# Long convolution with expert selection: eight places for x, a PSUM room, and two half blocks summed on VectorE

## The chip, the cores and the metric

One core of one Trainium2 chip. The metric is device time in microseconds (us) of one execution. The kernel before has a median of 868.43 us over three runs (866.48 to 869.74).

## What is computed

```python
def _attn_ref(x, v, pos_emb, w1, w2):
    h_mlp = np.maximum(pos_emb @ w1, 0.0) @ w2
    h_filt = h_mlp * np.exp(-0.01 * pos)[:, None]
    u = x * v
    Uf = np.fft.rfft(u, n=2 * S, axis=1)
    Hf = np.fft.rfft(h_filt, n=2 * S, axis=0)
    y = np.fft.irfft(Uf * Hf[None], n=2 * S, axis=1)[:, :S, :]
    return x * y                      # (4, 12608, 128), f32

def _moe_ref(x, w_gate, w1, w2, capacity):
    scores = np.einsum('bsd,d->bs', x, w_gate)
    out = x.copy()
    for b in range(B):
        top_idx = np.argpartition(-scores[b], capacity)[:capacity]
        ...
        out[b, top_idx] = x[b, top_idx] + g[:, None] * ye
    return out
```

The long convolution of `x * v` with a generated filter is multiplied by `x`. Every row of that product is given a score (its dot product with `w_gate`), the 128 best rows of each batch go through a small network, and their result is added to them.

## The kernel before

After the filter's transform (to about 106 us) the four batches are worked through in 128 groups of four channels, 32 groups per batch. A group goes through a forward transform (TensorE, lines L436 and L278), a product with the filter's transform (VectorE, L442 to L457, and GpSimd, L463 and L464) and a first backward transform (TensorE, L273), whose result ScalarE copies into the big tile `ay` (L487, L488). The loop over `t` keeps groups at several stages in flight: the backward transform belongs to group `t - 3`. So one turn of the loop issues, on TensorE, L273 of an old group, then L278 of group `t`, then L436 of group `t + 1`; on ScalarE L487 and L488, then L281 (the copy `qs` of one half of L278's result), then two L438.

After the last group of a batch the loop runs `P1.run`, called the run below: it finishes the batch. The batch has 16 blocks of 8 columns, worked in the order `ORD`, each as two half blocks `h` of 4 columns:

```python
HB = 4
LA = range(32 - 12, 32 - 2)
ORD = (0, 9, 1, 10, 2, 3, 11, 4, 12, 5, 6, 13, 7, 14, 8, 15)
NL, NM = 28, 7
DW = (2, 14)
```

For each half block TensorE makes the last backward transform into one of four PSUM tiles (`mm`, L553 and L557). VectorE multiplies it with x, in place of x (`fin`, L568). Then the product is multiplied with the gate's weights into a "room" `wx` (`weigh`, L602: on VectorE, or on GpSimd for the far columns), and ScalarE adds up each of the room's four columns with an activation that has an accumulator, in place (`sums`, L612): its result is the score of 128 rows. The rooms for VectorE's L602 are four, used in turn (`self.wx`): two in the arena's region `wx`, one in `te`, one in `ht`. The sums of the last four half blocks of a batch are kept for later (`late`) and issued in three lots by the next batch's first groups, behind the two L438 of a group; after them `mask` (L616) sets invalid scores aside and the selection of the 128 best begins, in the background of the next batch's groups. Its last step before it uses TensorE is a chain on VectorE (L616, L783, L779), then ScalarE (L780, L781). In the last batch nothing is late, and the last two half blocks (30, 31) are summed on VectorE itself by four `scalar_tensor_tensor` with an accumulator each (L586).

Where x lies: block number `i` of the order lies in place `i % 7`. Five places are a region of their own (`xa`), two (`XE`) lie over the buffers `qs` and `mt` of the groups. The first five blocks are loaded in halves ahead, one half in each of the groups `LA` (20 to 29) of the batch; two more when the run starts; and the load of block `i + 6` (L530) is issued by SyncE behind the store of block `i` (L591), and waits until the store of block `i - 1`, whose place it takes, has landed. SyncE issues all transfers of the kernel in one order, so a load that waits holds the stores behind it. Since `qs` and `mt` share bytes with the two `XE` places, the first L281 after a run waits for the store of the last block that lay in the first `XE` place: block number 12 of the order; VectorE's first L450 waits for the same.

Of the kernel before, what the change touches and what calls it, by code (L numbers as in the profile page):

```python
# [23 lines left out]
NG = 32  # L24
HC = 4 * N1
# [4 lines left out]
HB = 4  # L30
# [13 lines left out]
LA = range(32 - 12, 32 - 2)  # L44
# [8 lines left out]
DW = (2, 14)  # L53
OFF, _o = {}, 0
for _n, _k, _w in (("te", 2, 2 * HC), ("qs", 2, HC), ("mt", 1, 2 * HC), ("ws", 1, 888), ("yz", 2, 2 * HC), ("sd", 2, 2 * HC),
                   ("ht", NH, 2 * HC), ("xa", NX, 8 * D), ("wx", 2, HB * D), ("cm", 2, 2 * NC * D), ("x", NU, XC), ("", 1, 2), ("v", NV, XC)):
    OFF[_n] = (_o, _k, _w)
    _o += _k * _w
ARENA = _o
XE = [OFF["qs"][0] + k * 12 * D for k in range(2)]  # L60
CE = [o + 8 * D for o in XE]
POS0, HID0 = 0, PJ * N1
# [109 lines left out]
def hyena_moe(ctx, tc, xg, x2, pos, bw, ww, wg, mw1, mw2, fo, fc, c1, gx, cf, ci, wm, tk, out):  # L172
# [34 lines left out]
    def gap(k, n):  # L207
        return bank2[k].rearrange("p (c x) -> p c x", c=2)[:, :, HC:HC + n]
# [303 lines left out]
    class P1:  # L512
        def __init__(self, b):
            self.b = b
            self.sc = small([128, NJ], f"sc_{b}", tag="sc")
            self.xa, self.s4, self.cm = {}, {}, {}
            self.mul = None
            self.hbs = hbs
            self.more = iter(CB)
            self.pw = self.nw = 0  # L520
            self.late = []

        def load_a(self, i, a=0, z=8):
            if i < len(ORD):
                k = ORD[i]
                j0, j1 = blocks[k]
                z = min(z, j1 - j0)
                o = i % (NX + len(XE))
                self.xa[k] = buf("xa", o, [128, 8, D]) if o < NX else view(arena, XE[o - NX], [128, 8, D])
                nc.sync.dma_start(self.xa[k][P0:P0 + PR, a:z], x2[self.b, :, j0 + a:j0 + z])  # L530
# [29 lines left out]
        def fin(self, h):  # L560
# [4 lines left out]
            end = self.last and h >= len(self.hbs) - 2  # L565
# [3 lines left out]
            if not end:  # L569
                self.weigh()  # L570
                far = ja >= JM and h + 1 < len(self.hbs) and h not in DW
                if h >= NL and not self.last:
                    o = OFF["cm"][0] + 2 * NC * D if h < 30 else OFF["wx"][0]
                    wx = view(arena, o + h % 2 * HB * D, [128, HB, D])
                elif far:
                    wx = view(arena, CE[self.pw % 2], [128, HB, D])
                    self.pw += 1
                else:
                    wx = view(arena, self.wx[self.nw % 4], [128, HB, D])
                    self.nw += 1  # L580
# [3 lines left out]
            else:  # L584
                for k in range(n):
                    nc.vector.scalar_tensor_tensor(out=junk, in0=xa[:, ja % 8 + k], scalar=1.0,  # L586
                                                   in1=self.wg, op0=ALU.mult, op1=ALU.mult,
                                                   accum_out=self.sc[:, ja + k:ja + k + 1])
            if ja + n == blocks[blk][1]:
# [3 lines left out]
                if i:  # L593
                    self.load_a(i - 1 + NX + len(XE))
# [3 lines left out]
        def weigh(self):  # L598
            if self.mul:
# [3 lines left out]
                cols = [(wx[:, k], ja + k) for k in range(n)]  # L603
# [6 lines left out]
        def sums(self, cols):  # L610
            for x, j in cols:
                nc.scalar.activation(out=x, in_=x, func=AF.Copy, accum_out=self.sc[:, j:j + 1])  # L612

        def mask(self):
            sc, m = (self.sc, negm) if self.last else (c3(self.sc), negp)
            nc.vector.tensor_tensor(out=sc, in0=sc, in1=m, op=ALU.min)  # L616

        def run(self, ex):
            self.last = ex is not None
            self.ring = (0, 1, 2) if ex else (3, 2, 0, 1)  # L620
            self.wx = [OFF["wx"][0], OFF["wx"][0] + HB * D, OFF["te"][0] + (2 * HC if ex else 0),
                       OFF["sd"][0] if ex else OFF["ht"][0] + ((self.b + 1) * NG + 2) % NH * 2 * HC]
            self.wg = ps2(1, [128, D], f"wg_{self.b}")
            nc.scalar.copy(out=self.wg, in_=wgb)
            for k in range(len(XE)):
                self.load_a(NX + k)
# [452 lines left out]
    for t in range(NT + LAG):  # L1079
# [4 lines left out]
        if t < NT:  # L1084
# [12 lines left out]
            for k in range(2 * t, min(2 * t + 2, NX)):  # L1097
                nc.scalar.activation(out=buf("xa", k, [128, 8 * D]), in_=one.to_broadcast([128, 8 * D]), func=AF.Copy,
# [102 lines left out]
```

## Time and profile before

| what | us |
|---|---|
| median of three runs | 868.43 (866.48, 868.43, 869.74) |
| the profiled execution's own time | 866.19 |
| its span in the trace | 864.1 |
| busy: TensorE, VectorE, GpSimd, ScalarE | 829.2, 758.8, 719.4, 626.1 |

Starts are counted from the span's start, which covers 864.1 of the 866.19 us. The profiled execution lies 2.24 us under the median. L-numbers are lines of the kernel before. TensorE is listed twice on the page, as PE (products) and PEld (weight loads, which overlap the products). The runs lie at about 252 to 289, 430 to 467, 607 to 644 and 779 to 818 us; what follows them in the trace up to about 303, 480 and 660 us is called the seam here.

### The profile page before, as it was taken

How to read it: one execution, taken by the hardware profiler on the slowest of the kernel's cores; microseconds unless marked ns; L12 is line 12 of the kernel's file. 1: busy time of each engine (PE TensorE's matmuls, PEld its weight loads, DVE VectorE, ACT ScalarE, POOL GpSimd, SP SyncE). 2: the span in 40 equal slices, each digit the busy share in tenths (PEclk: the TensorE clock that was granted, in tenths of full speed). 3: DMA queues.
4: the chain of work that ended last, by engine and by line, in shares of the span. 5: the costliest groups of instructions: out<-in, count | busy, mean ns of one | idle time of the engine just before them, and what ended most of it. 6: DMA issues, size and time to landing. Idle time of an engine off the chain costs nothing.

```text
span 864.1 us, 45963 instructions
## 1 busy us (share of the span) xinstructions
PE 829.2 (96%) x19382; PEld 681.9 (79%) x19382; DVE 758.8 (88%) x1514; ACT 626.1 (72%) x2291; POOL 719.4 (83%) x837
## 2 busy tenths in 40 slices
PE   8999999999999999999999999999999999999875
PEld 5766668888889877777898777779997777779864
DVE  7999989999999789999996998999978989997873
ACT  6766575555559879885588898965797989657961
POOL 5799659999999689898997899989978989879610
PEclk9999999999999999999999999999999999999987
DMA  8044587777878967678779777787798767857810
GB/s 254 3 175 175 207 294 223 223 226 238 268 220 270 314 205 225 212 233 257 226 243 305 258 207 216 229 250 248 225 297 279 218 197 233 241 150 221 289 43 7
DMA packets 83134, 190.25 MB, mean 220 GB/s; under 512 B 9683, under 2 KB 46524, under 8 KB 82928
## 3 DMA queue, kind: packets, MB, share of 16 engines
q1 hardware_dynamic: 82672, 186.79, 68.5%
q8 instruction: 152, 2.49, 1.2%
q0 software_dynamic: 256, 0.52, 0.2%
q14 instruction: 54, 0.44, 0.2%
HBM read 147.57 MB, written 39.71 MB: 217 GB/s over the span
## 4 chain that ended last, share of the span: by engine, by line
PE 66%; DVE 15%; DMA 10%; ACT 5%; issue 3%; POOL 0%; SPq 0%; POOLq 0%; DVEq 0%; ACTq 0%
PE c L273 20%; PE c L278 15%; PE a L436 15%; DMA out_dram<-arena 8%; PE c L412 3%; PE a L393 3%; PE c L393 3%; ACT arena L612 2%; DMA arena<-in_x_dram 2%; DVE big L361 2%; DVE arena L450 2%; DVE c L451 2%; PE a L553 2%; PE a L557 1%; PE c L557 1%
## 5 line engine op out<-in xcount | busy, mean ns | idle before, releaser
L273 PE MATMUL c<-ci_sb,arena 128*23 128x128 f32 x8128 | 249.3, 273 | 5.1 <-issue 2.1
L273 PEld LDWEIGHTS c<-ci_sb,arena 128*23 128x23 f32 x8128 | 227.5, 103 | 14.1 <-issue 5.2
L278 PE MATMUL c<-arena,cf_sb 128*32 128x364 f32 x2048 | 183.5, 470 | 5.5 <-ACT arena L438 3.3
L436 PE MATMUL a<-cons,arena 128*32 128x182 f32 (+1 forms) x4096 | 185.6, 318 | 0.6 <-DVE arena L568 0.6
L436 PEld LDWEIGHTS a<-cons,arena 128*32 128x32 f32 (+1 forms) x4096 | 137.7, 110 | 44.3 <-issue 10.7
L487 ACT COPY big<-c 128x800 f32<-128x800 f32 x127 | 103.8, 817 | 80.7 <-PE c L273 80.2
L612 ACT ACTIVATE arena<-arena 128x128 f32<-128x128 f32 x504 | 148.0, 298 | 9.5 <-DVE arena L602 9.4
L463 POOL TENSOR_TENSOR arena<-arena 128x364 f32<-128x364 f32 x127 | 113.8, 896 | 48.1 <-DVE arena L457 42.3
L438 ACT COPY arena<-a 128x364 f32<-128x364 f32 x256 | 119.5, 467 | 42.4 <-PE a L436 37.8
L259 POOL TENSOR_TENSOR arena<-arena 128x508 f32<-128x508 f32 x128 | 139.1, 1087 | 8.6 <-DMA arena<-in_xg_dram 8.5
L450 DVE TENSOR_TENSOR arena<-c,arena 128x728 f32<-128x728 f32 x127 | 116.3, 915 | 3.8
L451 DVE TENSOR_TENSOR c<-c,arena 128x728 f32<-128x728 f32 x127 | 116.1, 914 | 0.0
L464 POOL TENSOR_TENSOR arena<-arena 128x364 f32<-128x364 f32 x127 | 114.3, 900 | 0.0
L278 PEld LDWEIGHTS c<-arena,cf_sb 128*32 128x32 f32 x2048 | 69.4, 110 | 51.3 <-issue 30.5
L612 ACT ACTIVATION_READ_ACCUMULATOR arena<-arena 128x1 f32 x504 | 95.5, 189 | 0.0
L445 DVE TENSOR_TENSOR c<-c,arena 128x364 f32<-128x364 f32 x128 | 69.6, 543 | 22.1 <-ACT arena L281 19.4
L507 POOL TENSOR_TENSOR big<-big,arena 128x224 f32<-128x224 f32 x128 | 74.4, 581 | 10.0
L540 POOL TENSOR_TENSOR arena<-big 128x512 f32<-128x512 f32 x64 | 79.7, 1276 | 0.6 <-PE a L553 0.3
L456 DVE TENSOR_TENSOR arena<-c,arena 128x364 f32<-128x364 f32 x127 | 68.2, 537 | 13.2 <-POOL big L506 0.5
L281 ACT COPY arena<-c 128x364 f32<-128x364 f32 x128 | 59.1, 462 | 24.1 <-DMA out_dram<-arena 7.4
L506 POOL TENSOR_TENSOR big<-big,arena 128x224 f32<-128x224 f32 x128 | 74.5, 582 | 0.0
L442 DVE TENSOR_TENSOR c<-c,arena 128x364 f32<-128x364 f32 x128 | 69.6, 544 | 2.6
(218 smaller groups left out, 1372.4 us busy)
## 6 DMA issues: line engine op xcount, KB each, us to landing
arena<-in_xg_dram SPq DMA_DIRECT2D x256, 254.0 KB, 3.5
arena<-hd SPq DMA_DIRECT2D x128, 364.0 KB, 4.1
out_dram<-arena SPq DMA_DIRECT2D x64, 420.0 KB, 6.0
arena<-in_x_dram SPq DMA_DIRECT2D x44, 420.0 KB, 4.9
hd<-arena SPq DMA_DIRECT2D x32, 364.0 KB, 2.8
arena<-in_x_dram SPq DMA_DIRECT2D x40, 210.0 KB, 4.6
arena<-in_pos_dram SPq DMA_DIRECT2D x16, 182.0 KB, 3.8
arena<-in_moe_w_dram SPq DMA_DIRECT2D x2, 512.0 KB, 4.7
```

The lines of the kernel that those rows point to most:

```text
L259: nc.gpsimd.tensor_tensor(out=x, in0=x, in1=v, op=ALU.mult)
L273: nc.tensor.matmul(o[32 * k:32 * k + c.stop - c.start], lhsT=lhsT[:, c], rhs=rhs, start=True, stop=True)
L278: nc.tensor.matmul(pq[w][a:a + 32], lhsT=cf_sb[:, 2 * w + a // NQ, a % NQ:a % NQ + 32], rhs=te[:, a // NQ], start=True, stop=True)
L436: nc.tensor.matmul(tps[s // 2][c, s % 2], lhsT=u[:, s, c], rhs=c1_sb[:, k], start=True, stop=True)
L438: nc.scalar.copy(out=te[:, :, 2 * h:2 * h + 2].rearrange("p e s i -> p s e i"), in_=tps[h])
L450: nc.vector.tensor_tensor(out=mt, in0=uv, in1=ht[:, 0].unsqueeze(1).to_broadcast([128, 2, HC]), op=ALU.mult)
L451: nc.vector.tensor_tensor(out=uv, in0=uv, in1=ht[:, 1].unsqueeze(1).to_broadcast([128, 2, HC]), op=ALU.mult)
L463: eng.tensor_tensor(out=nat(sd[:, 0]), in0=nat(yz[:, 0]), in1=rev(yz[:, 1]), op=ALU.add)
L464: eng.tensor_tensor(out=nat(sd[:, 1]), in0=rev(yz[:, 0]), in1=nat(yz[:, 1]), op=ALU.subtract)
L487: nc.scalar.copy(out=ay[:, t % NG, :NJ + JM, ss], in_=o3[:, :, :NJ + JM].rearrange("p s x -> p x s"))
L540: nc.gpsimd.tensor_tensor(out=cm[:, e].rearrange("p j (g s) -> p j g s", s=4), in0=av[0], in1=av[1], op=op)
L612: nc.scalar.activation(out=x, in_=x, func=AF.Copy, accum_out=self.sc[:, j:j + 1])
```

## The change

Eight places for x: the region `wx` (both its rooms) becomes place 0, the five of `xa` places 1 to 5, the two `XE` places 6 and 7. Six blocks are loaded ahead (in groups 18 to 29), two at the run's start, and block `i + 7` takes the place of block `i - 1`. The four rooms are now one in `te`, one in PSUM (the second half of `bank2[1]`), one in `ht` and one in the last `x` buffer (in the last batch `sd`). ScalarE's sums of a PSUM room write their unused result to one place in the arena, `sums_o`, all four of them. Half blocks 11 and 21 are weighed and summed by VectorE itself, with L586, into a small tile `sd` that `mask` copies to the scores. `gap` gives one contiguous piece of the first PSUM bank's gap where it gave two.

```diff
-LA = range(32 - 12, 32 - 2)
+LA = range(32 - 14, 32 - 2)
+DA = (11, 21)
+XP = [OFF["wx"][0], *(OFF["xa"][0] + k * 8 * D for k in range(NX)), *XE]
+NP0 = NX + 1
...
     def gap(k, n):
-        return bank2[k].rearrange("p (c x) -> p c x", c=2)[:, :, HC:HC + n]
+        return bank2[k][:, HC:HC + 2 * n].rearrange("p (c x) -> p c x", c=2)
...
+            self.sd = small([128, 4 * len(DA)], f"sd_{b}", tag="sd")
...
-                o = i % (NX + len(XE))
-                self.xa[k] = buf("xa", o, [128, 8, D]) if o < NX else view(arena, XE[o - NX], [128, 8, D])
+                self.xa[k] = view(arena, XP[i % len(XP)], [128, 8, D])
...
-            end = self.last and h >= len(self.hbs) - 2
+            end = h in DA or self.last and h >= len(self.hbs) - 2
...
-                    nc.vector.scalar_tensor_tensor(out=junk, in0=xa[:, ja % 8 + k], scalar=1.0,
+                    nc.vector.scalar_tensor_tensor(out=self.dva, in0=xa[:, ja % 8 + k], scalar=1.0,
                                                    in1=self.wg, op0=ALU.mult, op1=ALU.mult,
-                                                   accum_out=self.sc[:, ja + k:ja + k + 1])
+                                                   accum_out=self.own(h, ja)[:, k:k + 1])
...
-                    self.load_a(i - 1 + NX + len(XE))
+                    self.load_a(i - 1 + len(XP))
...
-                cols = [(wx[:, k], ja + k) for k in range(n)]
+                cols = [(wx[:, k], wx[:, k] if wx.tensor is arena.tensor else self.sums_o, ja + k) for k in range(n)]
...
-            for x, j in cols:
-                nc.scalar.activation(out=x, in_=x, func=AF.Copy, accum_out=self.sc[:, j:j + 1])
+            for x, o, j in cols:
+                nc.scalar.activation(out=o, in_=x, func=AF.Copy, accum_out=self.sc[:, j:j + 1])
+
+        def own(self, h, ja):
+            return self.sd[:, 4 * DA.index(h):4 * DA.index(h) + 4] if h in DA else self.sc[:, ja:ja + HB]
 
         def mask(self):
+            for k, h in enumerate(DA):
+                nc.vector.tensor_copy(out=self.sc[:, self.hbs[h][0]:self.hbs[h][0] + HB], in_=self.sd[:, 4 * k:4 * k + 4])
...
-            self.wx = [OFF["wx"][0], OFF["wx"][0] + HB * D, OFF["te"][0] + (2 * HC if ex else 0),
-                       OFF["sd"][0] if ex else OFF["ht"][0] + ((self.b + 1) * NG + 2) % NH * 2 * HC]
+            o = OFF["te"][0] + (2 * HC if ex else 0), OFF["sd"][0] if ex else OFF["ht"][0] + ((self.b + 1) * NG + 2) % NH * 2 * HC
+            self.wx = [view(arena, o[0], [128, HB, D]), view(bank2[1], 512, [128, HB, D]), view(arena, o[1], [128, HB, D]),
+                       view(arena, OFF["sd"][0] + 2 * HC if ex else OFF["x"][0] + (NU - 1) * XC, [128, HB, D])]
+            self.dva = view(arena, o[1] + HB * D, [128, D])
+            self.sums_o = view(arena, o[0] + HB * D, [128, D])
...
             for k in range(len(XE)):
-                self.load_a(NX + k)
+                self.load_a(NP0 + k)
...
-            for k in range(2 * t, min(2 * t + 2, NX)):
-                nc.scalar.activation(out=buf("xa", k, [128, 8 * D]), in_=one.to_broadcast([128, 8 * D]), func=AF.Copy,
+            for k in range(2 * t, min(2 * t + 2, NP0)):
+                nc.scalar.activation(out=view(arena, XP[k], [128, 8 * D]), in_=one.to_broadcast([128, 8 * D]), func=AF.Copy,
                                      scale=0.0)
```

SyncE's order at the end of the first run; a row is a line and its transfer, `x6` stands for six like it in succession, and in_xg is the next groups' input. Before:

```order
L591 DMA out_dram<-arena 105x1024
L530 DMA arena<-in_x_dram 105x1024
L591 DMA out_dram<-arena 105x1024
L530 DMA arena<-in_x_dram 105x1024
L591 DMA out_dram<-arena 105x1024 x6
L253 DMA arena<-in_xg_dram 128x508 x2
L263 DMA arena<-hd 128x728
```

and with the change (lines have moved down by three):

```order
L594 DMA out_dram<-arena 105x1024
L533 DMA arena<-in_x_dram 105x1024
L594 DMA out_dram<-arena 105x1024 x7
L256 DMA arena<-in_xg_dram 128x508 x2
L266 DMA arena<-hd 128x728
```

The last load of a run stands one store earlier: behind the store of block number 8, where it stood behind that of number 9, and every load of the run is one block further on than the load that stood in its place.

VectorE's order around half block 11 of the first run; a_70, a_71, c_72 and c_74 are the PSUM tiles of the transform, c_73 is the first PSUM bank, which holds the weights. Before:

```order
L568 TENSOR_TENSOR arena<-c_72,arena 128x512
L602 TENSOR_TENSOR arena<-arena,c_73 128x512
L568 TENSOR_TENSOR arena<-a_70,arena 128x512
L602 TENSOR_TENSOR arena<-arena,c_73 128x512
L568 TENSOR_TENSOR arena<-a_71,arena 128x512
L602 TENSOR_TENSOR arena<-arena,c_73 128x512
L568 TENSOR_TENSOR arena<-c_74,arena 128x512
```

and with the change:

```order
L571 TENSOR_TENSOR arena<-c_72,arena 128x512
L605 TENSOR_TENSOR c_73<-arena,c_73 128x512
L571 TENSOR_TENSOR arena<-a_70,arena 128x512
L605 TENSOR_TENSOR arena<-arena,c_73 128x512 x2
L571 TENSOR_TENSOR arena<-a_71,arena 128x512
L589 SCALAR_TENSOR_TENSOR arena,sd_2979<-arena,c_73 128x128 x4
L571 TENSOR_TENSOR arena<-c_74,arena 128x512
```

L568 of half block 11 (a_71) is now followed by its four accumulations instead of standing between two L602, and the L602 before it comes earlier; one L602 writes into PSUM.

VectorE's order at the mask of the first batch, some turns into the next. Before:

```order
L442 TENSOR_TENSOR c_73<-c_73,arena 128x364
L616 TENSOR_TENSOR sc_3127<-sc_3127,c_73 128x128
L783 TENSOR_SCALAR c_72<-sc_3127 128x2x64
L779 TENSOR_TENSOR sc_3127<-sc_3127,c_72 128x128
L450 TENSOR_TENSOR arena<-c_73,arena 128x728
```

and with the change:

```order
L445 TENSOR_TENSOR c_73<-c_73,arena 128x364
L622 COPY sc_2978<-sd_2979 128x4 x2
L624 TENSOR_TENSOR sc_2978<-sc_2978,c_73 128x128
L794 TENSOR_SCALAR c_72<-sc_2978 128x128
L790 TENSOR_TENSOR sc_2978<-sc_2978,c_72 128x128
L453 TENSOR_TENSOR arena<-c_73,arena 128x728
```

Two small copies stand ahead of the mask and its chain. The orders of TensorE and GpSimd are as they were.

What waits: with eight places the last block in the first `XE` place is number 14 of the order (`i % 8 == 6`), and in the second number 15. So the first L281 and the first L450 after a run now wait for the store of block number 14, where they waited for number 12; the first L456 (`yz`) for number 15, where it waited for number 13.

## Rows read from the trace of the kernel before

**Rows 1.** Page, part 1: busy time, share of the span, instructions.

```profile
PE 829.2 (96%) x19382; PEld 681.9 (79%) x19382; DVE 758.8 (88%) x1514; ACT 626.1 (72%) x2291; POOL 719.4 (83%) x837
```

**Rows 2.** Timeline of PE, undisturbed groups: start, duration, what, [idle before <- releaser].

```profile
172.40 1.96 PE L273 MATMUL c<-ci_sb,arena 128*23 128x128 f32 x64
176.60 1.96 PE L273 MATMUL c<-ci_sb,arena 128*23 128x128 f32 x64
```

**Rows 3.** Timeline of PE: first and third L273 after each of three runs.

```profile
289.24 1.95 PE L273 MATMUL c<-ci_sb,arena 128*23 128x128 f32 x64
...
299.21 2.11 PE L273 MATMUL c<-ci_sb,arena 128*23 128x128 f32 x61 [0.43 <-ACT arena L488]
...
468.33 1.95 PE L273 MATMUL c<-ci_sb,arena 128*23 128x128 f32 x64 [0.98 <-DVE arena L568]
...
477.95 0.31 PE L273 MATMUL c<-ci_sb,arena 128*23 128x128 f32 x4 [0.29 <-ACT arena L488]
...
644.70 1.95 PE L273 MATMUL c<-ci_sb,arena 128*23 128x128 f32 x64 [0.22 <-DVE arena L568]
...
655.20 1.07 PE L273 MATMUL c<-ci_sb,arena 128*23 128x128 f32 x32 [0.42 <-ACT arena L488]
```

**Rows 4.** Timeline of ACT: the first L281 after each of three runs.

```profile
294.74 0.46 ACT L281 COPY arena<-c 128x364 f32<-128x364 f32 x1 [2.41 <-DMA out_dram<-arena]
...
473.48 0.46 ACT L281 COPY arena<-c 128x364 f32<-128x364 f32 x1 [2.06 <-DMA out_dram<-arena]
...
650.73 0.46 ACT L281 COPY arena<-c 128x364 f32<-128x364 f32 x1 [2.94 <-DMA out_dram<-arena]
```

**Rows 5.** Timeline of DVE, L568 at the ends of three runs (x2: half blocks 28, 29).

```profile
285.60 0.69 DVE L568 TENSOR_TENSOR arena<-a,arena 128x512 f32<-128x512 f32 x1 [1.07 <-DMA arena<-in_x_dram]
...
287.74 1.29 DVE L568 TENSOR_TENSOR arena<-c,arena 128x512 f32<-128x512 f32 x2 [0.25 <-DMA arena<-in_x_dram]
...
291.41 0.69 DVE L568 TENSOR_TENSOR arena<-a,arena 128x512 f32<-128x512 f32 x1 [1.79 <-DMA arena<-in_x_dram]
...
467.58 1.29 DVE L568 TENSOR_TENSOR arena<-c,arena 128x512 f32<-128x512 f32 x2 [2.11 <-DMA arena<-in_x_dram]
...
643.95 1.29 DVE L568 TENSOR_TENSOR arena<-c,arena 128x512 f32<-128x512 f32 x2 [1.22 <-DMA arena<-in_x_dram]
```

**Rows 6.** Timeline of SP, end of run one; then the landing of L591, 283 to 294.

```profile
286.49 0.34 SPq L530 DMA_DIRECT2D arena<-in_x_dram  x1
286.87 7.15 SPq L591 DMA_DIRECT2D out_dram<-arena  x6
...
DMA to landing us min/median/max: 5.6/6.1/6.9
```

**Rows 7.** Stretches: length, busy PE PEld DVE ACT POOL, PEclk, DMA share, GB/s.

```profile
283.00:289.00 6.00, 6.00 (x114) 6.00 (x112) 4.43 (x8) 6.00 (x42) 3.35 (x4) 1.00 0.91 289
462.00:468.00 6.00, 5.35 (x98) 5.10 (x94) 3.21 (x6) 6.00 (x42) 3.73 (x4) 1.00 0.90 283
639.00:645.00 6.00, 5.78 (x114) 5.54 (x112) 3.63 (x7) 6.00 (x43) 3.77 (x4) 1.00 0.91 291
289.00:295.00 6.00, 5.67 (x158) 4.21 (x158) 3.20 (x6) 2.92 (x15) 3.56 (x5) 1.00 0.93 343
```

**Rows 8.** Timeline of DVE: half block 30 of the last run, and its first accumulation.

```profile
817.16 0.69 DVE L568 TENSOR_TENSOR arena<-a,arena 128x512 f32<-128x512 f32 x1 [0.88 <-DMA arena<-in_x_dram]
817.96 0.29 DVE L586 SCALAR_TENSOR_TENSOR arena<-arena,c 128x128 f32<-128x128 f32 x1
```

**Rows 9.** Page, part 5: ScalarE's sums (busy, mean ns, idle before).

```profile
L612 ACT ACTIVATE arena<-arena 128x128 f32<-128x128 f32 x504 | 148.0, 298 | 9.5 <-DVE arena L602 9.4
...
L612 ACT ACTIVATION_READ_ACCUMULATOR arena<-arena 128x1 f32 x504 | 95.5, 189 | 0.0
```

**Rows 10.** PE's wait behind the mask's chain (timeline); a small operation of DVE (groups by form).

```profile
311.79 1.43 PE L278 MATMUL c<-arena,cf_sb 128*32 128x364 f32 x16 [0.23 <-ACT c L781]
...
L726 DVE TENSOR_SCALAR st<-cons 128x4 f32<-128x4 f32 x2 | 0.5, 225 | 0.0
```

**Rows 11.** Timeline of ACT: the zeroing of a place for x.

```profile
118.32 1.06 ACT L1098 ACTIVATE arena<-cons 128x1024 f32<-128x1024 f32 x1
```

More of the change, by code (lines that the diff above doesn't have):

```diff
@@ L53 @@
 DW = (2, 14)
+DA = (11, 21)
 OFF, _o = {}, 0
 for _n, _k, _w in (("te", 2, 2 * HC), ("qs", 2, HC), ("mt", 1, 2 * HC), ("ws", 1, 888), ("yz", 2, 2 * HC), ("sd", 2, 2 * HC),
-                   ("ht", NH, 2 * HC), ("xa", NX, 8 * D), ("wx", 2, HB * D), ("cm", 2, 2 * NC * D), ("x", NU, XC), ("", 1, 2), ("v", NV, XC)):
+                   ("ht", NH, 2 * HC), ("xa", NX, 8 * D), ("wx", 2, HB * D), ("cm", 2, 2 * NC * D), ("x", NU, XC), ("", 1, 6), ("v", NV, XC)):
     OFF[_n] = (_o, _k, _w)
@@ L578, in fin @@
                 else:
-                    wx = view(arena, self.wx[self.nw % 4], [128, HB, D])
+                    wx = self.wx[self.nw % len(self.wx)]
                     self.nw += 1
```

## The prediction

> **What bounds the kernel now.** I read the page's busy times first, then PE's timeline where it is not full, then who released it there. TensorE is busy 96% of the span, with no other engine above 88% [rows 1]; so only the few places where it waits can give anything, and no engine's total matters. An undisturbed group takes 176.60 − 172.40 = 4.20 us of PE [rows 2]. Of the seams, look at the first and the third L273 after a run: they should be 2 × 4.20 = 8.40 apart. In the first seam they are 9.97 apart (1.57 too many), in the second 9.62 (1.22), in the third 10.50 (2.10), and the second and third seam begin late by 0.98 and 0.22, waiting for VectorE's L568 [rows 3]. All this together is 6.09 us: what a perfect seam would give back, three times summed.
>
> Two late things stand behind that, and the reader should keep them apart. **Late x:** L568 of the last half blocks waits for the load of x, 1.07 + 0.25 + 1.79 in the first run and 2.11 and 1.22 at half block 28 of the next two [rows 5]. **Late stores:** the first L281 after each run waits 2.41, 2.06 and 2.94 for a store to land, and starts at 294.74, 473.48 and 650.73 [rows 4]. The second comes later than the first, and it is the one that holds the third L273: ScalarE goes from that L281 through two L438 and seven late sums to L487 and L488, and the third L273 is released by L488 [rows 3]. So x being early is worth only what it does to the landing of one store.
>
> In the last run nothing follows but the selection of the last batch, which nothing covers; there L568 of half block 30 waits 0.88 for x [rows 8], and that is lost outright.
>
> **The change part by part.**
>
> *Eight places.* Each load of the run moves one place up in SP's queue, so the last one leaves in the slot of the one before it, a store earlier, and SP's hold at 286.49 (the load that waits for a landing, with six stores issued behind it in 7.15 us [rows 6]) no longer stands between stores 9 and 10. One block (two halves, in groups 18 and 19) is loaded ahead instead. I cost those two at nothing: PE there runs at its undisturbed 4.20 [rows 2], and later halves of the same kind go beside the same work now. The waits of L568 for x then go. But the first L281 now waits for store 14 instead of store 12. What matters is when store 14 lands, and that I bound from both sides.
>
> Early end: store 14 holds half blocks 28 and 29. Their L568 ended at 289.03 in the first run; without the 1.07 and 0.25 ahead of them 287.71. In the second it ended at 468.87, less 2.11 is 466.76; in the third 645.24, less 1.22, 644.02 [rows 5]. A store takes 5.6 to 6.9 us to land here, 6.1 in the median [rows 6]. With 6.1, and 0.1 to the copy, L281 starts at 293.9, 473.0 and 650.2: earlier by 0.8, 0.5 and 0.5, together 1.85; with 5.6 it is 3.35.
>
> Late end: stores queue behind each other. One more transfer of 420 KB (430,080 bytes) lies between the last load and the store that is waited for (five stores instead of three, and the load itself a slot earlier), at 343 GB/s 1.25 us [rows 7]. Against it stands the lull that SP's hold leaves: in the six us before the bulk of stores the DMA moves 289, 283 and 291 GB/s instead of 343 [rows 7], which is 0.94, 1.05 and 0.91 us of transfer that can be filled. So L281 comes 0.31, 0.20 and 0.34 later, together 0.85.
>
> The ends are +3.35 and −0.85; neither row is nearer, since the queue and the latency both act, so I take the middle: **−1.25 us** for the three seams.
>
> The Trainium skill, "DMA: Bandwidth & Descriptors", section "Queues, rings and completion order", says that on each DMA engine descriptors are consumed in ring order, while completion need not be in order. By it store 14 cannot begin ahead of 10 to 13, which is the late end, and the seams would cost 0.85 instead of giving 1.25. No row here shows a store that overtakes another.
>
> *The tail.* L568 of half block 30 loses its wait of 0.88, which the row puts down to the load alone [rows 8]: **−0.9 us**.
>
> *Rooms.* The L602 that writes PSUM is the same 128x512 operation. ScalarE's sums of that room all write one place, so each waits for the last: at most 298 + 189 = 487 ns where one activation now follows the other within about 298 [rows 9], 0.19 × 16 = 3.0 us a run. Half blocks 11 and 21 take eight sums from ScalarE, 8 × 0.298 = 2.4. Net at most +0.6, and ScalarE waits over 2 us for a store at the end of each run anyway [rows 4]: nothing. If the store were early, those 0.6 would be late next.
>
> *Half blocks 11 and 21 on VectorE.* Four accumulations of 0.29, 1.16 and a little for reading the accumulators [rows 8], replace one L602, which I take at the pace of L568, half of 1.29 [rows 5]: +0.5 and up, I take 0.7 each. VectorE is not full in the run's end (4.43 of 6.00 [rows 7]), and the load's waits that go leave it 3.1 us in the first. Nothing; if that cover were gone, +1.5 a run on VectorE.
>
> *The copies before the mask.* Two operations of 128x4; the nearest row is 0.225 [rows 10], in succession perhaps 0.15. They lie on a chain that TensorE waits for in each of three batches (0.23 in the first [rows 10]), so they go straight to its wait: 3 × 0.2 to 0.3 less what cover there is, **+0.6** (0 to 1.3).
>
> *One more place zeroed.* One activation of 1.06 [rows 11], in a stage where ScalarE still has idle time: **+0.2** (0 to 1.0).
>
> *The gap* is the same elements in one piece: nothing.
>
> Sum: −1.25 − 0.9 + 0.6 + 0.2 = −1.35. Against the profiled execution's own 866.19 that is 864.84; that execution lies 2.24 under the median, and the same step from the median of 868.43 gives **867.1**.
>
> **The rivals.**
>
> *The seams become whole.* Stores come so early that L281 waits for nothing; then all 6.09 are won, with the tail and the two costs −6.2: 862.2. For it: late x is what delays the run's stores, and it goes. Against: that needs L281 some 1.7 us earlier or more in every seam, beyond the early end above.
>
> *The stores become the wait* (slower). The copy waits for a store two blocks further on, in a queue that is full already (0.91 [rows 7]); if the lulls aren't filled, each seam pays the full transfer, 3 × 1.25 = 3.75, and −0.9 + 0.8 makes +3.65: 872.1. It decides if stores 10 to 14 land evenly some 1.25 apart and the last load's landing is no earlier than the one that stood in its slot. For it: the share of 0.91; against: 343 GB/s are reached right after. The ring order that the Trainium skill's page above states is what would make it so.
>
> *It doesn't do what it says.* If bandwidth and not places makes x late, L568 waits as before and the tail too; then only the costs remain, +0.8: 869.2. For it: the same share of 0.91; against: the loads are issued after waiting for a landing, which eight places move.
>
> **How the numbers follow.** About 0.5%, 4.3 us, is what can be told from no change here; so faster is below 864.1 and slower above 872.8. Chances: the forecast 0.47, whole seams 0.20, stores 0.18, no effect 0.15. Faster: nearly all of the second and a little of the first, 0.24. Slower: the upper part of the third and a little of the others, 0.10. Same: 0.66. The forecast's own bounds are −3.35 − 0.9 = −4.25 to +0.85 − 0.9 + 2.3 = +2.3; reaching into the second and third case, the range is 861.8 to 872.2.
>
> **What would show it.** Right: L568's waits for x in the seams and at half block 30 gone; SP issues seven stores in succession; L281 still waits for a store, and starts within 1 us of where it did, counted from the run's first L273; the third L273 8.4 + 0.6 to 2 us after the first. Two copies of about 0.15 to 0.2 ahead of the mask, and PE's wait for L781 longer by as much. Wrong: L281 waiting for TensorE instead of a store (whole seams), L281 over a us later (stores), or L568 still waiting for x.

## The result, and the profile after

The changed kernel takes 878.79 us (877.99 to 880.1, six runs) against 867.45 for the kernel before, measured beside it: a ratio of 1.0125, 95% interval 1.0091 to 1.016 (estimated over all runs, here and below; it need not be the quotient of the two medians). It is slower by 1.25%, and the time lies above the forecast range. The profiled execution's span grew from 864.1 to 877.0, by 12.9 us. One execution of a later run, of 2180.37 us, is in the slow state and left out of the medians and ratios.

What was forecast to go did go. VectorE's waits for x, 12.1 us in 13 places over the whole trace of before, have no line left among its waits (what took them away, the places or the longer runs, the first experiment tells). The line of before (total, times, longest):

```profile
DVE arena L568 <- DMA arena<-in_x_dram: 12.1, 13, 2.1
```

SP, at the end of the first run, issues seven stores in succession (timeline; start, duration):

```profile
285.26 0.49 SPq L533 DMA_DIRECT2D arena<-in_x_dram  x1
285.81 10.61 SPq L594 DMA_DIRECT2D out_dram<-arena  x7
```

Most of the loss is inside the runs. From the last forward transform ahead of the first run to the first behind it, 41.19 us (249.81 to 291.00) have become 44.85. In PE's timeline of before, then of after, these are:

```profile
249.81 1.43 PE L278 MATMUL c<-arena,cf_sb 128*32 128x364 f32 x16
...
291.00 1.41 PE L278 MATMUL c<-arena,cf_sb 128*32 128x364 f32 x16
```

```profile
250.47 1.43 PE L281 MATMUL c<-arena,cf_sb 128*32 128x364 f32 x16
...
295.32 1.41 PE L281 MATMUL c<-arena,cf_sb 128*32 128x364 f32 x16
```

The other two runs went from 42.83 and 41.64 to 44.94 and 44.85: 9.0 us for the three. PE, which had nothing to wait for in a run, now waits for VectorE's product; VectorE waits for ScalarE's sums. The waits of VectorE and of PE, 250 to 305 us of after (total, times, longest):

```profile
DVE arena L605 <- ACT arena L615: 7.2, 4, 2.7
DVE c L448 <- ACT arena L284: 2.4, 3, 1.9
```

```profile
PE a L556 <- DVE arena L571: 1.2, 1, 1.2
PE a L560 <- DVE arena L571: 1.2, 1, 1.2
PE c L276 <- ACT arena L491: 0.4, 1, 0.4
PE c L556 <- DVE arena L571: 0.4, 1, 0.4
```

Over the trace to 700 us the first of these is 21.6 us in 12 waits, four a run; before it does not exist. One of the four, in the timelines of VectorE, ScalarE and PE:

```profile
266.53 0.69 DVE L605 TENSOR_TENSOR c<-arena,c 128x512 f32<-128x512 f32 x1
267.12 0.68 DVE L571 TENSOR_TENSOR arena<-a,arena 128x512 f32<-128x512 f32 x1
270.49 1.29 DVE L605 TENSOR_TENSOR arena<-arena,c 128x512 f32<-128x512 f32 x2 [2.69 <-ACT arena L615]
```

```profile
268.62 0.29 ACT L615 ACTIVATE arena<-arena 128x128 f32<-128x128 f32 x1
...
268.91 0.25 ACT L615 ACTIVATE arena<-c 128x128 f32<-128x128 f32 x1
...
270.09 0.28 ACT L615 ACTIVATE arena<-c 128x128 f32<-128x128 f32 x1
270.26 0.19 ACT L615 ACTIVATION_READ_ACCUMULATOR arena<-c 128x1 f32 x1
```

```profile
272.43 1.09 PE L560 MATMUL a<-big,cons 128*64 128x128 f32 x16 [1.24 <-DVE arena L571]
```

Read them together. At 266.53 VectorE fills the PSUM room. ScalarE is behind with other rooms until 268.9, then sums the PSUM room, from 268.91 to 270.45. At 267.8 VectorE could go on to the next room, which is in the arena, long summed and free; it stands still until the fourth sum of the PSUM room is done. PE's four PSUM tiles are full by then, and PE stands still for 1.24 us until 272.43. The next room is not what VectorE waits for: it reads the gate's weights from the same PSUM tile as the room lies in, and the program orders that read behind ScalarE's reads of the room (the run that changes only this read shows it, below). With all rooms in the arena ScalarE could be several half blocks behind, and before has no such wait; with this one VectorE waits four times a run for ScalarE's whole backlog.

Behind the runs the forecast is nearly met. The first L284 (before: L281) still waits for a store:

```profile
298.23 0.46 ACT L284 COPY arena<-c 128x364 f32<-128x364 f32 x1 [1.58 <-DMA out_dram<-arena]
...
479.03 0.46 ACT L284 COPY arena<-c 128x364 f32<-128x364 f32 x1 [2.65 <-DMA out_dram<-arena]
...
658.76 0.46 ACT L284 COPY arena<-c 128x364 f32<-128x364 f32 x1 [1.69 <-DMA out_dram<-arena]
```

Counted from the first L276 after each run (293.56, 473.28, 653.98) it starts at 4.67, 5.75 and 4.78 us; before, from [rows 3, 4], at 5.50, 5.15 and 6.03. The third L276 stands 9.14, 10.22 and 9.26 behind the first, where 9.97, 9.62 and 10.50 were read. Together that is 1.5 us less, where 1.25 was forecast. But the runs are longer here, so the stores have more time, and the agreement may be luck; what eight places do alone is for the experiments.

Two smaller terms. The copies before the mask take up to four times what was assumed, and PE's wait behind them grew from 0.23, 0.65 and 0.40 to 0.67, 1.04 and 1.53 (VectorE's and PE's timelines after, first and third batch):

```profile
312.10 0.23 DVE L622 COPY sc<-sd 128x4 f32<-128x4 f32 x2
...
672.64 0.97 DVE L622 COPY sc<-sd 128x4 f32<-128x4 f32 x2
```

```profile
313.85 1.43 PE L281 MATMUL c<-arena,cf_sb 128*32 128x364 f32 x16 [0.67 <-ACT c L792]
...
675.13 1.43 PE L281 MATMUL c<-arena,cf_sb 128*32 128x364 f32 x16 [1.53 <-ACT c L792]
```

That is 1.96 us together, for a term of 0.6 with a bound of 1.3. And from the last forward transform to the end it is 98.16 us where it was 95.23: the wait for x at half block 30 is gone, but VectorE waits 4.0 us for ScalarE's sums in the last run too, and from that last forward transform to the run's last product on TensorE it is 51.87 where it was 47.24.

### The profile page after: what moved, and what is told of

Read it like the earlier page. It is cut to its first block, busy times and chain, and to the rows that moved or that the text cites. A ratio compares the mean times of both kernels' runs of the same rounds, so it can differ in the third digit from the quotient of the medians.

```text
span 877.0 us, 45962 instructions
## 1 busy us (share of the span) xinstructions
PE 829.4 (95%) x19382; PEld 681.3 (78%) x19382; DVE 762.2 (87%) x1578; ACT 622.8 (71%) x2228; POOL 720.5 (82%) x837
## 4 chain that ended last, share of the span: by engine, by line
PE 64%; DVE 18%; DMA 6%; ACT 6%; issue 3%; POOL 2%; SPq 0%; POOLq 0%; DVEq 0%; ACTq 0%
PE c L276 18%; PE c L281 14%; PE a L439 14%; DMA out_dram<-arena 4%; ACT arena L615 4%; PE c L415 3%; PE a L396 3%; PE c L396 3%; DVE arena L453 2%; DVE c L454 2%; PE c L560 2%; PE a L556 2%; DVE arena L571 2%; DVE big L364 2%; PE c L556 2%
## 5 line engine op out<-in xcount | busy, mean ns | idle before, releaser
L276 PE MATMUL c<-ci_sb,arena 128*23 128x128 f32 x8128 | 249.4, 273 | 3.4 <-ACT arena L491 1.3
L276 PEld LDWEIGHTS c<-ci_sb,arena 128*23 128x23 f32 x8128 | 227.6, 103 | 12.3 <-issue 5.4
L281 PE MATMUL c<-arena,cf_sb 128*32 128x364 f32 x2048 | 182.6, 470 | 8.3 <-ACT c L792 3.2
L466 POOL TENSOR_TENSOR arena<-arena 128x364 f32<-128x364 f32 x127 | 114.1, 898 | 52.2 <-DVE arena L460 43.6
L615 ACT ACTIVATE arena<-arena 128x128 f32<-128x128 f32 x408 | 120.0, 297 | 29.1 <-DVE arena L605 18.5
L467 POOL TENSOR_TENSOR arena<-arena 128x364 f32<-128x364 f32 x127 | 114.7, 903 | 0.0
L281 PEld LDWEIGHTS c<-arena,cf_sb 128*32 128x32 f32 x2048 | 69.2, 110 | 53.4 <-issue 30.5
L448 DVE TENSOR_TENSOR c<-c,arena 128x364 f32<-128x364 f32 x128 | 69.5, 543 | 25.5 <-ACT arena L284 22.2
L543 POOL TENSOR_TENSOR arena<-big 128x512 f32<-128x512 f32 x64 | 79.5, 1277 | 0.3 <-PE c L556 0.2
L615 ACT ACTIVATION_READ_ACCUMULATOR arena<-arena 128x1 f32 x408 | 76.8, 188 | 0.0
L284 ACT COPY arena<-c 128x364 f32<-128x364 f32 x128 | 59.2, 462 | 23.4 <-PE c L281 7.4
L605 POOL TENSOR_TENSOR arena<-arena,wgb 128x512 f32<-128x512 f32 x47 | 51.0, 1097 | 28.0 <-DVE arena L571 19.5
```

The costliest lines, as they stand in the source:

```text
L276: nc.tensor.matmul(o[32 * k:32 * k + c.stop - c.start], lhsT=lhsT[:, c], rhs=rhs, start=True, stop=True)
L281: nc.tensor.matmul(pq[w][a:a + 32], lhsT=cf_sb[:, 2 * w + a // NQ, a % NQ:a % NQ + 32], rhs=te[:, a // NQ], start=True, stop=True)
L466: eng.tensor_tensor(out=nat(sd[:, 0]), in0=nat(yz[:, 0]), in1=rev(yz[:, 1]), op=ALU.add)
L467: eng.tensor_tensor(out=nat(sd[:, 1]), in0=rev(yz[:, 0]), in1=nat(yz[:, 1]), op=ALU.subtract)
L543: nc.gpsimd.tensor_tensor(out=cm[:, e].rearrange("p j (g s) -> p j g s", s=4), in0=av[0], in1=av[1], op=op)
L615: nc.scalar.activation(out=o, in_=x, func=AF.Copy, accum_out=self.sc[:, j:j + 1])
```

## The experiments

Theory 1: the PSUM room, through the order just described, is the loss. Theory 2: the first copy after a run waits for a store two blocks further on. Theory 3: half blocks 11 and 21 overload VectorE. All ratios are to the kernel before, run beside it; its median was 869.12 us beside the PSUM room alone, the half blocks alone, the weights from SBUF and the PSUM room left out, 867.12 beside the sums in place, the loosened order and the last run, and 870.20 beside the other three. The diffs are cuts: they show the lines that make the difference.

**One part alone: the PSUM room in the kernel before.**

```diff
-            self.wx = [OFF["wx"][0], OFF["wx"][0] + HB * D, OFF["te"][0] + ...
+            self.wx = [view(arena, o[0], [128, HB, D]), view(bank2[1], 512, [128, HB, D]),
+                       view(arena, o[1], [128, HB, D]), view(arena, o[2], [128, HB, D])]
+            self.sums_o = view(arena, OFF["wx"][0] + HB * D, [128, D])
```

(`o` holds the other three rooms' places.)

> The kernel before, with one thing taken from the change: one of the four rooms (the second of the region wx) lies in PSUM beside the gate's weights, and the gap is one piece. Seven places, no half block summed on VectorE. Theory 1 (the PSUM room: each L602 of the room after it waits until ScalarE has done all four sums of the PSUM room): most of the loss is here, about 7 us of such waits in each run, 44 to 45 us from the last L278 ahead of a run to the first behind it instead of 41.2 to 42.8, and 874 to 880 us. Theory 2 (store 14 instead of store 12 holds the first L281): this kernel has seven places, so 866 to 870 us. Theory 3 (VectorE overloaded by half blocks 11 and 21): 866 to 870 us.

Measured: 881.82 us, ratio 1.0155 (1.0115 to 1.0195); the runs take 44.9 to 45.1 us. Its waits of VectorE in the first run:

```profile
DVE arena L602 <- ACT arena L612: 8.1, 4, 2.7
```

This part alone makes the whole loss; theories 2 and 3 had said no change. Not all of it is in the runs: from the last forward transform to the end it is 103.50 us, where before took 95.23. And VectorE's waits for x are gone from this trace as well, though it has seven places: the longer runs do that by themselves.

**One part alone: half blocks 11 and 21 on VectorE, in the kernel before.**

```diff
+DA = (11, 21)
-            end = self.last and h >= len(self.hbs) - 2
+            end = h in DA or self.last and h >= len(self.hbs) - 2
```

(and with it the accumulations into `sd` and the two copies ahead of the mask)

> The kernel before, with half blocks 11 and 21 weighed and summed on VectorE into the tile sd, and the two copies ahead of the mask; seven places, four rooms in the arena. Theory 1 (PSUM room): 866 to 870 us, the copies costing under 1 us. Theory 2 (stores): 866 to 870 us. Theory 3 (VectorE overloaded): PE waits for L568 during the run as in the changed kernel, some 3 us a run, 874 to 880 us.

Measured: 870.35, ratio 1.0021 (1.0 to 1.0042). Theory 3 falls: about 2 us, far from its 874, and the size of PE's longer wait behind the copies ahead of the mask (1.96 above). From one last forward transform ahead of a run to the third behind it (the run and two turns), the three seams are 1.8 longer, 1.4 shorter and 1.8 longer than before, though neither places nor stores were touched: one trace tells a seam only to some 2 us.

**The weights from SBUF.**

```diff
-                eng, w = (nc.gpsimd, wgb) if far else (nc.vector, self.wg)
+                eng, w = (nc.gpsimd, wgb) if far else (nc.vector, wgb)
```

(and the same in the accumulation)

> The changed kernel, with VectorE reading the gate's weights from SBUF (the copy GpSimd uses) in L605 and L589, so that nothing but the room itself is read from that PSUM tile. Theory 1 (PSUM room): L605 no longer waits for sums of the half block just ahead, the runs fall to 41 to 42.5 us, 862 to 870 us. Theory 2 (stores): the runs' length does not matter and the time stays at 874 to 880 us, with the first L281 after a run late. Theory 3 (VectorE overloaded): stays at 874 to 880 us, PE waiting for L571 in the runs.

Measured: 895.88, ratio 1.0294 (1.0249 to 1.034), runs of 49.2 to 49.6 us. The time lies above what any theory had. The waits of VectorE for ScalarE's sums are gone in the first run, as theory 1 had it, but the time went the other way, for another reason: VectorE's and GpSimd's operations became slower (that line's instructions, ns min/median/max; first the changed kernel, then this one).

```profile
L605 DVE TENSOR_TENSOR arena<-arena,c x14: 674/676/687, 257.6 to 296.1; 128x512 f32<-128x512 f32 x14
```

```profile
L605 DVE TENSOR_TENSOR arena<-arena,wgb x13: 674/1145/1753, 257.9 to 299.1; 128x512 f32<-128x512 f32 x13
```

So this run's time decides nothing between the theories; it shows what the weights in PSUM are good for.

**The order kept, the sums written in place.**

```diff
-                cols = [(wx[:, k], wx[:, k] if wx.tensor is arena.tensor else self.sums_o, ja + k) for k in range(n)]
+                cols = [(wx[:, k], wx[:, k], ja + k) for k in range(n)]
```

> The changed kernel with one edit: ScalarE's sums of the PSUM room write their unused result in place, into PSUM, not all four to one place in the arena, so a sum no longer waits for the sum ahead of it. VectorE's L605 of the next room still waits for all four. If the waiting of the sums on each other (one each 0.40 us instead of 0.29) is what makes PSUM dear, VectorE's four waits of a run fall from 7.2 us to under 5, and the time to 868 to 873 us. If the order between VectorE's read of the weights and ScalarE's sums is, the waits stay at 5.5 to 7 us and the time at 874 to 879 us.

Measured: 877.32, ratio 1.0136 (1.01 to 1.0172), and VectorE's waits in the first run:

```profile
DVE arena L605 <- ACT c L615: 7.3, 4, 2.7
```

Unchanged. But the edit did not free the sums from each other, as it was meant to: with four separate places to write they still follow each other every 0.40 us, in every one of the 48 places of this trace where one PSUM sum follows another.

```profile
267.53 0.26 ACT L615 ACTIVATE c<-c 128x128 f32<-128x128 f32 x1
...
267.94 0.26 ACT L615 ACTIVATE c<-c 128x128 f32<-128x128 f32 x1
```

So this run does not separate the two explanations; it shows that the shared place is not what spaces the sums. Against 0.29 for a sum in the arena, 0.11 more for 16 sums is 1.8 us a run, and VectorE waits 7.2. The next run decides.

**The order loosened by one half block.**

```diff
-                eng, w = (nc.gpsimd, wgb) if far else (nc.vector, self.wg)
+                eng, w = (nc.gpsimd, wgb) if far else (nc.vector, wgb if wx0 is self.keep else self.wg)
```

(`keep` is the room after the PSUM room)

> The changed kernel; only the L605 of the room that follows the PSUM room reads the weights from SBUF, the others from PSUM. So it is not the next L605 but the one after it that waits for the PSUM room's sums, one to two half blocks later; up to seven L605 of a run read the weights where GpSimd reads them. If the order with the sums is the loss, the waits fall from 7.2 us to 0 to 3 us a run and the runs from 44.9 to 42 to 43 us: 866 to 873 us. If reading SBUF beside GpSimd is what costs (as where all of VectorE's half blocks did it, 49 us a run), runs of 44 us or more, 875 us or more.

Measured: 873.85, ratio 1.0076 (1.005 to 1.0101). The waits for the sums fall from 21.6 to 5.1 us over three runs, the runs to 42.1, 44.1 and 43.0 us, by 5.4 of the 9.0. The line of VectorE's waits to 700 us:

```profile
DVE arena L606 <- ACT arena L616: 5.1, 6, 2.4
```

The sums of the PSUM room follow each other every 0.40 us here too. With the room and its sums unmoved and only the reader of its tile changed, over a third of the loss goes: it is the order with the read of the weights, and not the spacing of the sums. (The second run and the time, 0.85 us past its range, stay longer than this theory had it.)

**The PSUM room left out.**

```diff
-            self.wx = [view(arena, o[0], [128, HB, D]), view(bank2[1], 512, [128, HB, D]), view(arena, o[1], [128, HB, D]),
+            self.wx = [view(arena, o[0], [128, HB, D]), view(arena, o[1], [128, HB, D]),
```

> The changed kernel with the PSUM room left out: three rooms in the arena, eight places, half blocks 11 and 21 on VectorE. Theory 1 (PSUM room): the waits of 1.0 to 2.7 us go; with three rooms VectorE may wait for a room's own sums three uses earlier, so 864 to 873 us. Theory 2 (stores): 874 to 880 us. Theory 3 (VectorE overloaded): 874 to 880 us.

Measured: 874.99, ratio 1.0062 (1.0036 to 1.0089). Half of the loss goes, and theory 1 is right about the runs: 41.27, 41.33 and 41.22 us, with no wait of VectorE for sums and one of 1.4 us for x, three rooms being enough. But now theory 2 shows, which the longer runs had covered. The first L284 waits 12.7 us in the three seams together, before 7.4 [rows 4]:

```profile
294.39 0.46 ACT L284 COPY arena<-c 128x364 f32<-128x364 f32 x1 [2.40 <-DMA out_dram<-arena]
...
474.69 0.46 ACT L284 COPY arena<-c 128x364 f32<-128x364 f32 x1 [4.97 <-DMA out_dram<-arena]
...
656.21 0.46 ACT L284 COPY arena<-c 128x364 f32<-128x364 f32 x1 [5.34 <-DMA out_dram<-arena]
```

The first two turns after the second and third run take 13.6 and 13.9 us; before they took 9.6 and 10.5. Run and two turns together are 0.1 us shorter than before in the first seam, 2.5 and 2.9 longer in the others. The copy itself starts 5.49, 8.06 and 8.43 us after the first L276, where before had 5.50, 5.15 and 6.03. In the last two seams TensorE has stood nearly idle behind that wait (0.27 of 3.50 us busy from 472.5, 0.85 of 3.50 from 654.0), and then its granted clock is 0.50, the lower of its two levels; the forward transform takes 2.30 and 2.66 us there instead of 1.41 (stretches of 1 us: length, busy PE PEld DVE ACT POOL, granted clock, DMA share, GB/s):

```profile
477.00:478.00 1.00, 1.00 (x12) 0.33 (x8) 1.00 (x2) 1.00 (x9) 0.00 (x0) 0.50 0.97 358
...
658.00:659.00 1.00, 1.00 (x12) 0.40 (x8) 1.00 (x2) 1.00 (x9) 0.00 (x0) 0.50 0.99 343
```

So a part of what the late store costs here, up to about 1 us in each of those second turns (5.91 and 5.80 where 4.83 is usual), comes by way of the clock.

**The shared places moved within the eight (three rooms, as in the run before).**

```diff
-XP = [OFF["wx"][0], *(OFF["xa"][0] + k * 8 * D for k in range(NX)), *XE]
+XA = [OFF["wx"][0], *(OFF["xa"][0] + k * 8 * D for k in range(NX))]
+XP = [*XA[:4], *XE, *XA[4:]]
+PRE, NOW = (0, 1, 2, 3, 6, 7), (4, 5)
```

(and the loads and the zeroing follow these numbers)

> Three rooms in the arena, eight places, half blocks 11 and 21 on VectorE, as in the run with three rooms; but the two places that share bytes with qs and mt are numbers 4 and 5 of the eight, not 6 and 7 (blocks 0 to 3, 6 and 7 are loaded ahead, 4 and 5 at the run's start). So the first L281 after a run waits for the store of block number 12 again, the first L456 for 13. Theory A (what is left of the loss without the PSUM room is the store that L281 waits for): its waits of 2.4, 5.0 and 5.3 us fall to 0 to 1.5, the four turns after a run come to 18 to 19.5 us, 862 to 868 us. Theory B (all stores are late, whichever is waited for, since the DMA is full): the waits stay over 3 us in the second and third seam, 871 to 876 us.

Measured: 868.16, ratio 0.9985 (0.9956 to 1.0015), where three rooms without this edit had 1.0062. The waits that the trace puts down to a store fall from 12.7 to 2.9 us, the longest 2.2. In the second seam the copy waits 2.88 and starts 5.97 us after the first backward transform, where an undisturbed one starts at 3.24:

```profile
472.29 0.46 ACT L286 COPY arena<-c 128x364 f32<-128x364 f32 x1 [2.88 <-PE c L278]
```

The copy does not read the product named there, and the forward transform that it reads was done by 469.5; a store is the likelier, and then 5.8 us are left of 12.7. The four turns come to 18.5, 20.6 and 20.0 us. So it is theory A in kind, and short of it in size: time, waits and two of the three seams lie past the late end of what it expected.

**The same without half blocks on VectorE.**

```diff
-DA = (11, 21)
+DA = ()
```

> The same with half blocks 11 and 21 back on the common way (L605 and ScalarE's sums), so no copies ahead of the mask. If the half blocks on VectorE help (three rooms are then used less, ScalarE has eight sums fewer), this is slower than the run with them by 1 to 5 us; if they cost (copies on the mask's chain, VectorE's time), it is 1 to 3 us faster.

Measured: 865.77, ratio 0.9965 (0.9939 to 0.9992); with them it was 0.9985, and the intervals overlap. Together with the 1.0021 above, the two half blocks on VectorE cost rather than help, by about 2 us. Store waits are uneven from run to run: here one of 5.1 us stands in the second seam.

**The kernel before, with the shared places as numbers 3 and 4 of its seven.**

```diff
+XP = [*XA[:3], *XE, *XA[3:]]
+PRE, NOW = (0, 1, 2, 5, 6), (3, 4)
```

(`XA` is here the five places of `xa`.)

> The kernel before (seven places, four rooms) with the two places that share bytes with qs and mt as numbers 3 and 4 of the seven: blocks 0, 1, 2, 5 and 6 are loaded ahead, 3 and 4 at the run's start, and the first L281 after a run waits for the store of block number 11 where it waited for 12 (block 11 is the last in place 4; L281 and L450 touch the place of block 10, L456 that of 11). Theory A (the store that L281 waits for is the loss of the seams): L281's waits of 2.4, 2.1 and 2.9 us go, and 2 to 5 us of time with them, 864 to 867 us. Theory C (late x is the loss): L568's waits for x stay and so does the time, 868 to 870 us.

(The store that L281's place waits for is that of block number 10, as the bracket says.) Measured: 866.76, ratio 0.9967 (0.9946 to 0.9988). The waits for stores are gone (0.3 us left of 7.4), L568's for x stay, and with them runs of 41.9 to 42.9 us where an undisturbed one takes 41.2. So the wait for the store costs something by itself. Taken away alone, here, it leaves the waits for x; the waits for x taken away alone, in the run with three rooms, leave the store.

**Both taken away: eight places, three rooms, no half block on VectorE, the shared places as numbers 3 and 4.**

```diff
+XP = [*XA[:3], *XE, *XA[3:]]
+PRE, NOW = (0, 1, 2, 5, 6, 7), (3, 4)
-DA = (11, 21)
+DA = ()
```

> Eight places, three rooms in the arena, no half block summed on VectorE, and the places that share bytes with qs and mt are numbers 3 and 4 of the eight: the first L281 after a run waits for the store of block number 11. If that store's landing is what is left in the seams (5.1 us of wait in the second seam of the run with numbers 4 and 5), the wait falls under 1 us in each seam and the time to 861 to 865 us; if transfers are late as a whole, L573 waits for x instead, and it is 865 to 868 us.

Measured: 860.47 against 867.12, ratio 0.9932 (0.9905 to 0.9959); this beats both kernels. All runs take 41.2 us, the waits for x come to 0.2 us in the whole trace, those for a store to 0.5. PE's first three backward transforms after the first run stand at an undisturbed distance of 4.2:

```profile
290.54 1.95 PE L278 MATMUL c<-ci_sb,arena 128*23 128x128 f32 x64
...
294.76 1.93 PE L278 MATMUL c<-ci_sb,arena 128*23 128x128 f32 x64
...
298.96 1.93 PE L278 MATMUL c<-ci_sb,arena 128*23 128x128 f32 x64
```

From the last forward transform to the end it is 92.47 us against 95.23.

## Why the prediction was wrong

**Rooms.** This is the step that failed. It costed the L602 that writes PSUM as the same operation, and counted only that the sums wait for each other, at most 0.6 us net on ScalarE, hidden. What it left out is a wait that the new room adds on another engine: VectorE's next read of the weights, in the same PSUM tile, behind ScalarE's four sums. That measured 21.6 us of VectorE's waits over three runs and 9.0 us of the runs' length, and alone, in the kernel before, 1.55%. The step also took ScalarE's slack at a run's end as cover, where the wait takes in ScalarE's backlog in the middle of a run. And it did not ask what stands behind a new wait: VectorE's products do, and PE's four tiles wait for those. The one cost that was seen is not the one that counts: sums in PSUM follow each other every 0.40 us instead of 0.29, so 0.11 more and not up to 0.19, and with that spacing kept the waits fall to 5.1 us when one reader of the weights is moved. Its reason, four sums writing one place, did not hold either: written in place they keep the same 0.40.

**Eight places.** In the changed kernel all 12.1 us of VectorE's waits for x went, but with the PSUM room alone and seven places they went too. The mechanism is seen where the runs take 41.2 us: with three rooms and eight places 1.4 us are left, so it was right. What the places are worth was bounded at a gain of 3.35 and a loss of 0.85, with the middle taken. Three rooms in the arena, with no wait for sums in the run, are the nearest thing to a test of the term, and there run and two turns come to −0.1, +2.5 and +2.9, together 5.3 us longer: beyond the late end. Single seams scatter by some 2 us, and the lower clock has a part in it, so the size is rough; but the copy's lateness comes to 5.3 as well, 1.8 a seam, and moving the shared places alone brings the ratio from 1.0062 to 0.9985. So without the PSUM room the rival of the stores, priced at 1.25 a seam, would have been the case. The section of the Trainium skill's page "DMA: Bandwidth & Descriptors" that was cited for it, "Queues, rings and completion order", has descriptors consumed in ring order on each DMA engine. The trace with three rooms agrees as far as it goes: in its second seam store 10 landed at 469.9 us and store 14, behind it in the queue, at 474.6, 0.1 before the copy. In the changed kernel itself this did not show, because the longer runs gave the stores time; L281 (there L284) started within 1.25 us of where it did, about as forecast, and that was luck: the sum had no longer runs in it, and without them the term has the other sign. The result came out on the side of that rival, but not by its mechanism.

**Whole seams.** The 6.09 us summed for a perfect seam were real: with both waits taken away the three runs with two turns behind each take 6.45 us less in the trace, and the kernel is 6.65 us faster in the medians, tail included. What the prediction said against this rival, that more places cannot by themselves bring L281 early enough, also held: it took a change of which store it waits for.

**The tail.** The wait of 0.88 at half block 30 went, as forecast: from the last run's last product on TensorE to the end of VectorE's last L568 it is 2.89 us instead of 3.75, shorter by 0.86. VectorE's waits for sums in the last run, 4.0 us, cover it up. That the places did it is not shown: 2.78 stands in the runs with three rooms and eight places, but also in the one with seven places and the shared ones moved. Whole stretches to the end do not show a term of this size, since the selection behind them (from the mask to TensorE's last product) takes 36.5 to 40.6 us in these traces.

**The smaller terms.** Half blocks 11 and 21 on VectorE cost about 2 us in two comparisons, one of which reaches nothing at its interval's end, in the other the two intervals overlap; the size is that of the copies, which were mis-sized: 0.23 to 0.97 for the pair, and 1.96 us of PE's wait instead of 0.6. The turn behind the zeroing of one more place became 5.25 us where it was 4.31, 0.9 rather than 0.2; it is 5.25 or 5.26 in every trace with eight places and 4.31 in every one with seven, so the place added, by its zeroing as far as these runs can tell, is the cause. Counted from the starts of the forward transforms, the 12.9 us are +9.0 in the runs, −1.6 in the two turns behind each, −1.7 in the third turn behind the first (4.33 where it was 6.04, not counted in the prediction), +1.7 in the turns of the mask, +0.9 here and +2.9 from the last forward transform to the end. What remains, some 1.7 us spread over the later groups, was not followed up.

## What to carry to other kernels

Before a buffer is put beside something in one PSUM tile, list who reads that tile: an engine that only reads the neighbour can be ordered behind another engine's work on the buffer, and then it waits for that engine's whole backlog. Where two late things end close together, taking one away can bring out the other; price a cure by what is left when both have gone, and ask which transfer the next stage waits for, not only when its own data comes. A resource can often be given to the waiter by renaming which place is used when, at no cost in space.

## What was not expected of the hardware

VectorE's 128x512 product with weights from SBUF, beside GpSimd's work, took 1145 ns in the median and up to 1753, against 676 with the weights in PSUM; the 128x128 accumulation 730 instead of 287; and GpSimd's L543 1706 instead of 1270, in the same runs. VectorE's long ones lie beside GpSimd's operations: of the four accumulations of half block 21, the three that begin while L543 works take 0.64 and 1.23 us, the one behind its end (290.80) takes 0.29 (VectorE, then GpSimd):

```profile
288.44 1.23 DVE L589 SCALAR_TENSOR_TENSOR arena<-arena,wgb 128x128 f32<-128x128 f32 x1
...
289.72 1.23 DVE L589 SCALAR_TENSOR_TENSOR arena<-arena,wgb 128x128 f32<-128x128 f32 x1
...
290.99 0.29 DVE L589 SCALAR_TENSOR_TENSOR arena<-arena,wgb 128x128 f32<-128x128 f32 x1
```

```profile
284.87 5.93 POOL L543 TENSOR_TENSOR arena<-big 128x512 f32<-128x512 f32 x4
```

The copies ahead of the mask, from SBUF to SBUF, show the same: one takes 0.16 us, and in the last batch, with nothing on GpSimd, both do; the long one of the second batch takes 0.42 and ends at 493.31, that of the third 0.90 and ends at 673.61, each 0.02 us behind the end of a GpSimd operation that had begun before it (L466 and L467). Not every copy beside GpSimd is long: in the first batch both took 0.16. That is what the 0.2 to 0.3 assumed for a pair left out.

A sum on ScalarE that reads PSUM took 250 to 280 ns, not 290 to 300, but in a PSUM room the sums follow each other every 0.40 us instead of 0.29, whether they write one place in the arena or their own in PSUM. What spaces them was not found.
